# Probability times v in native fp32 for all 32 attention items, native scores for 4 items instead of 8

## The chip, the cores and the metric

The kernel runs on one core of one Trainium2 chip. The metric is device time in microseconds (us) from launch to end, as the median of several executions. A core has a matrix engine (TensorE, called PE in the rows; its weight loads are PEld), a vector engine (VectorE, DVE), a scalar engine (ScalarE, ACT), a third elementwise engine (GpSimd, POOL) and a sync engine (SyncE, SP), which here issues the transfers. Each engine runs its own list of instructions strictly in the order in which the program gives them and waits on semaphores for the others.

## The reference

Three stages follow each other: block-causal attention over 4 batches with 8 heads, 576 positions and a head width of 64, then two feed-forward layers on the 2304 tokens.

```python
scores = scale * np.matmul(q, k.transpose(0, 1, 3, 2))
mask = block_i >= block_j            # blocks of 64 positions
scores = np.where(mask, scores, -1000000000.0)
scores = scores - np.max(scores, axis=-1, keepdims=True)
attn = np.exp(scores)
attn = attn / (np.sum(attn, axis=-1, keepdims=True) + 1e-09)
x = np.matmul(attn, v)               # back to (2304, 512)
h = np.maximum(np.maximum(x @ w1, x @ w2), x @ w3)      # 512 -> 768
x = h @ w_out                                           # 768 -> 512
h = x @ w_in                                            # 512 -> 2048
out = (h * np.cos(h)) @ w_out2                          # 2048 -> 512
```

## The kernel before, in words

**Two ways to multiply.** A product of fp32 numbers is either made natively (both operands fp32; one matmul in the program is two passes in the trace) or from three products of fp32r parts: each operand is split into a high part (a cast to fp32r) and a low part (the rest), and high times high, low times high and high times low are added up in PSUM. The split costs a cast and a subtraction on ACT or DVE for each operand.

**Items.** Attention is cut into 32 items: batch, half, pair of heads. The low half of a batch has the query positions 0 to 319 (5 blocks of 64, keys in 3 tiles of 128), the high half the positions 320 to 575 (4 blocks, keys in 5 tiles). Items 0 to 3 are the low half of batch 0 (one for each pair), items 4 to 7 its high half, items 8 to 11 the low half of batch 1, and so on. The two heads of a pair stand side by side: rows 0 to 63 and 64 to 127.

**An item's steps.** `prep` splits q and k (tiles `qbd`, `kh`, `kl`) and v (`vs`) into parts. `scores` multiplies (PSUM tile `S`, one buffer), takes the row maximum (DVE, `stat`), the exponential (ACT, `prob`, one buffer for all items), the reciprocal of the row sums (DVE) and scales `prob`. `transposes` turns `prob` on PE (`tb`) and copies it to `pt`, as high and low part. `pv` multiplies v by `pt` into `X` and writes the result as high and low part (`xhi`, `xlo`), from which the first feed-forward layer reads.

**Native items.** The first 8 items (`NATIVE = 8`) do without any split: q is put by a transfer into a block-diagonal tile `qnat` (pool `cv_start`), scores are native, `pt` is one fp32 tile, and `pv` makes 64-column native matmuls, head 0 into rows 0 to 63 of `X`, head 1 into rows 64 to 127. For the other 24 items `pv` loads 128 columns of v parts, works on one head after the other, and adds the partial sums up in a tile `x32` (rows with `x<-X`).

**Weights.** `convert` takes a weight tile from its 64-bit words to high and low parts: about four DVE instructions of 128x512 (rows with `t`, then `wlo` or `vlo`) and one to three on either engine. 24 of them (`w1`, `w2`, `w3`, `wout`) are needed by the first layer.

**The first layer** (`moe1_units`) is a queue of units for each half of a batch: 18 groups of 12 matmuls (`psm<-xhi,whi` and the like, 4 units each) and 4 groups of 18. A group fills one of two PSUM banks (`ps_m`), which is emptied to a tile `hm` of the pool `wk`. The pool `wk` is opened in the place of `cv_start` (`R.close(cv_start)`, `wk = R.open(cv_start, ...)`): it comes into being when the last instruction that touches a tile of `cv_start`, `qnat` among them, is through.

**The order** of each engine's instructions is the work of a planner (class `Plan`): it records all instructions, prices them (`price`, `spent`), schedules the list forwards and backwards several times and emits the best order. `with R.unit()` makes several matmuls one piece that is not torn apart. The prices set only the order.

Of the kernel before, what the change touches and what calls it, by code (L numbers as in the profile page):

```python
# [8 lines left out]
F32 = mybir.dt.float32  # L9
F32R = mybir.dt.float32r  # L10
# [4 lines left out]
ALU = mybir.AluOpType  # L15
# [4 lines left out]
P = 128  # L20
NLOW, NHIGH = 320, 256
# [4 lines left out]
def f32(ap):  # L26
    return ap.bitcast(F32)
# [101 lines left out]

class Plan:  # L130
    CROSS = 150.0
    COLD = 30000.0
    EARLY = 130000.0
    WEIGHT = {"DVE": 2.5, "ACT": 1.0, "POOL": 100.0}

    def __init__(self, tc):
# [106 lines left out]
    def price(self, engine, method, outs, ins, kw):  # L243


        if engine == "SP":
            tiles = outs + ins
            return 600.0, 2000.0 + sum(v.n * v.rows * 4 for v in tiles[:1]) / 240.0, False
        n = outs[0].n
        if engine == "PE":  # L250
            late = 190.0
            if method == "transpose":
                return 109.0, late, False
            dt = ins[0].buf.dt
            if dt == F32:
                return 4 * n / 2.4 + 13, late, False
            load = ins[0].n / 1.2
            return (max(n / 2.4 + 3, 65.0) if dt == BF16 else max(n / 2.4 + 13.5, load)), late, False
        psum = any(v.buf.psum for v in outs + ins)
        if method == "tensor_reduce":  # L260
            n = ins[0].n
        spread = 120.0 * (outs[0].hi - outs[0].lo + 1 > n)
        if engine == "ACT":
            scaled = isinstance(kw.get("scale"), View)
            return (n * 0.833 + spread + (55 if psum else 100) + 95 * ("bias" in kw) + 95 * scaled
                    + 93 * ("accum_out" in kw)), 112.0, False
        if engine == "DVE":
            sb = [v for v in ins if not v.buf.psum]
            fast = method in ("tensor_copy", "tensor_scalar", "memset") and not psum
            two = method in ("tensor_tensor", "scalar_tensor_tensor") and len(sb) > 1  # L270
            if method == "reciprocal":
                return 70.0 + 5 * n, 100.0, False
            return n * (0.52 if fast else 1.04) + 68 + spread, 88.0, fast or two
        return (n * 3.3 + 75 if method == "tensor_tensor" else max(400.0, n * 1.04 + 195)), 45.0, method != "memset"
# [5 lines left out]
    def after(self, d, o, stop):  # L280
        if d.engine == "PE" and o.engine == "PE":
            return -d.late
        if d.engine == "CTL" or o.engine == "CTL":
            return 0.0
        return self.CROSS if stop > self.EARLY else 35.0

    def spent(self, o, start):
        return o.cost * (2 if o.engine == "PE" and start < self.COLD else 1)

    def forward(self, rank):  # L290

# [14 lines left out]
        def release(o):  # L306
# [5 lines left out]
            if o.ways:  # L312
                def done(way):
                    e, (cost, late, shared), _ = way
                    start = max(free[e] + load[e], at)
                    if shared:
                        start = max(start, port)
                    return start + cost * self.WEIGHT[e] + late
                chosen[o] = min(o.ways, key=done)
# [121 lines left out]
def fused_kernel(tc, qk, v2, w1, w2, w3, wout, w_in2, w_out2, out):  # L441
# [11 lines left out]
    R = Plan(tc)  # L453
# [7 lines left out]
    at = R.open(name="at", bufs=1, side="right")  # L461
    ps_x = R.open(name="ps_x", bufs=1, space=PSUM, side="right")
# [49 lines left out]
    for u in range(2):  # L512
        f = Half()
# [9 lines left out]
            ((4, 0, 0, 320, 1), (2, 0, 320, 192, 1), (3, 1, 0, 256, 1), (1, 1, 256, 128, 1), (0, 1, 384, 64, 1)),)  # L523
        HALF.append(f)
    POFF = {6: 0, 8: 4, 5: 9, 7: 12, 2: 2, 4: 6, 0: 16, 1: 0, 3: 4}
    NATIVE = 8

    items = []
    for b in range(B):
        for half in range(2):  # L530
            for pair in range(HP):
                it = Item()
                it.b, it.half, it.pair, it.n, it.f = b, half, pair, len(items), HALF[half]
                it.native = it.n < NATIVE
                items.append(it)
# [32 lines left out]
    def prep(it):  # L568
        f = it.f
        if it.native:  # L570
            return
        nb, nk = len(f.blocks), f.nk
        kh = it.kh = at.tile([P, S], F32R, "kh", tag="kh")[:, :nk]
        kl = it.kl = at.tile([P, S], F32R, "kl", tag="kl")[:, :nk]
        R.copy(kh, it.k)
        R.sub(kl, it.k, f32(kh))
        for a in (0, 64):
            q = it.q[a:a + 64].rearrange("p (b n) -> p b n", n=64)
            hi, lo = (t[a:a + 64, 0:nb, a:a + 64] for t in qbd)
            R.scale(hi, q, scale)  # L580
            R.vector.scalar_tensor_tensor(lo, q, scale, f32(hi), ALU.mult, ALU.subtract)
        vs = it.vs = at.tile([P, 5, 4, 64], F32R, "vs", tag="vs")
        js = slice(0, f.nj)
        R.copy(vs[:, js, 0:4:3], it.vr[:, js])
        R.sub(vs[:, js, 1:3], it.vr[:, js], f32(vs[:, js, 0:4:3]))

    def scores(it):

# [3 lines left out]
        for tile_ in f.tiles:  # L592
# [15 lines left out]
            for b, b0, c0, n, c in tile_:  # L608
                i = b - f.first
                part = s[:, :, c0:c0 + n] if c == 2 else s[:, b0, c0:c0 + n]  # L610
                R.vector.tensor_reduce(st[:, i:i + 1], part, axis=AX.XY if c == 2 else AX.X, op=ALU.max, negate=True)
                bias = st[:, i:i + 1]
# [15 lines left out]

    def transposes(it):
        order = it.f.order  # L630
        it.pt = at.tile([P, 2, 16, P], F32 if it.native else F32R, "pt", tag="pt")
        for c in range(0, len(order), 4):
            part = order[c:c + 4]
            n = P * len(part)
            t = ps_x.tile([P, 512], F32, "tb", tag="T", bufs=2)
            with R.unit():
                for x, (j, b) in enumerate(part):
                    o = (POFF[b] + j) * P
                    R.tensor.transpose(t[:, x * P:x * P + P], prob[:, o:o + P], ident)
            hi, lo = (it.pt[:, i, c:c + len(part)].rearrange("p b n -> p (b n)") for i in range(2))  # L640
            R.copy(hi, t[:, :n])
            if not it.native:
                R.vector.tensor_tensor(lo, t[:, :n], f32(hi), ALU.subtract)

    def pv(it):
        f = it.f
        n = f.n
        h, l = xhi[it.half][:, it.pair], xlo[it.half][:, it.pair]
        where = {}
        for c, (j, b) in enumerate(f.order):  # L650
            where.setdefault(j, []).append((c, b))
        if it.native:
            X = ps_x.tile([P, 512], F32, "X", tag="X", bufs=2)
        else:
            x32 = at.tile([P, NLOW], F32, "x32", tag="x32")
        for e in range(2):
            a, o = 64 * e, 64 - 64 * e
            if not it.native:
                X = ps_x.tile([P, 512], F32, "X", tag="X", bufs=2)
            for j in range(f.nj):  # L660
                c0, b0 = where[j][0]
                nb = len(where[j])
                q0 = 64 * (b0 - f.first)
                if not it.native and q0 >= f.both:

                    v = it.vs[:, j, 2 * e:2 * e + 2].rearrange("p a d -> p (a d)")
                    dst = X[:, f.both:2 * n - f.both].then(
                        lambda ap, q=q0 - f.both: ap.rearrange("p (c q) -> p c q", c=2)[:, :, q:])
                    dst.n = 2 * (n - q0)
                    R.tensor.matmul(dst, v, it.pt[:, :, c0:c0 + nb, a:a + 64], start=j == 0, stop=j == f.nj - 1,  # L670
                                    skip_group_check=True)
                    continue
                with R.unit():
                    for i in range(1 if it.native else 2):
                        p = it.pt[:, i, c0:c0 + nb, a:a + 64]
                        if it.native:
                            R.tensor.matmul(X[a:a + 64, q0:n], it.vr[:, j, e], p, start=j == 0,
                                            stop=j == f.nj - 1, skip_group_check=True)
                        else:
                            v = it.vs[:, j, 2 * e:2 * e + 2].rearrange("p a d -> p (a d)")  # L680
                            R.tensor.matmul(X[:, q0:n], v, p, start=j == 0 and i == 0, stop=j == f.nj - 1 and i == 1,
                                            skip_group_check=True)
            if not it.native:
                R.scalar.copy(x32[a:a + 64, :n], X[o:o + 64, :n])
                R.vector.tensor_tensor(x32[a:a + 64, :n], X[a:a + 64, :n], x32[a:a + 64, :n], ALU.add).cost += 118.0
                R.vector.tensor_tensor(x32[a:a + 64, f.both:n], X[a:a + 64, n:2 * n - f.both], x32[a:a + 64, f.both:n],
                                       ALU.add).cost += 118.0
        if it.native:
            R.copy(h, X[:, :n])
            R.vector.tensor_tensor(l, X[:, :n], f32(h), ALU.subtract)  # L690
        else:
            R.copy(h, x32[:, :n])
            R.sub(l, x32[:, :n], f32(h))


    bank_pools = [(ps_m, 2)]
# [106 lines left out]
    for n in range(NI + 1):  # L803
# [3 lines left out]
        for step in range(3):  # L807
# [4 lines left out]
            if step == 2 and n:  # L812
                it = items[n - 1]
# [122 lines left out]
    for n in range(len(seq) + LAG):  # L936
        if n < len(seq):
            c, fc = seq[n]
# [62 lines left out]
```

## Time and profile before

| | |
|---|---|
| median of 3 runs | 929.67 us (929.02 to 930.89) |
| the profiled execution | 929.6 us, its span from first to last instruction 927.5 us |
| PE busy | 899.2 us of the span (97%) |
| DVE, ACT busy | 662.7 us (71%), 478.7 us (52%) |
| mean granted clock | 0.994 |

The span is 2.1 us shorter than the execution's own time. The table's busy times include the latency of each instruction, so an engine that looks nearly full can still have room.

### The profile page before, as it was taken

How to read it: one execution, taken by the hardware profiler on the slowest of the kernel's cores; microseconds unless marked ns; L12 is line 12 of the kernel's file. 1: busy time of each engine (PE TensorE's matmuls, PEld its weight loads, DVE VectorE, ACT ScalarE, POOL GpSimd, SP SyncE). 2: the span in 40 equal slices, each digit the busy share in tenths (PEclk: the TensorE clock that was granted, in tenths of full speed). 3: DMA queues.
4: the chain of work that ended last, by engine and by line, in shares of the span. 5: the costliest groups of instructions: out<-in, count | busy, mean ns of one | idle time of the engine just before them, and what ended most of it. 6: DMA issues, size and time to landing. Idle time of an engine off the chain costs nothing.

```text
span 927.5 us, 14314 instructions
## 1 busy us (share of the span) xinstructions
PE 899.2 (97%) x5388; PEld 801.7 (86%) x5388; DVE 662.7 (71%) x1402; ACT 478.7 (52%) x1080; POOL 0.7 (0%) x7
## 2 busy tenths in 40 slices
PE   6888999999999999999999999999999999999998
PEld 5656989999999999999999988888888888888897
DVE  6979868999889887677776899855555555455554
ACT  5867457776767765766664553442224223322233
POOL 0000000000000000000000000000000000000000
PEclk9899999999999999999999999999999999999999
DMA  7455332442443421212003592220001000100010
GB/s 218 151 156 170 116 136 92 149 160 95 135 138 113 144 66 39 64 34 89 15 1 123 179 370 96 58 78 14 1 1 69 0 1 1 46 1 0 1 46 23
DMA packets 39492, 78.51 MB, mean 85 GB/s; under 512 B 9728, under 2 KB 20992, under 8 KB 39424
## 3 DMA queue, kind: packets, MB, share of 16 engines
q1 hardware_dynamic: 39424, 77.61, 25.3%
q8 instruction: 42, 0.69, 0.3%
q14 instruction: 26, 0.21, 0.1%
HBM read 61.34 MB, written 16.25 MB: 84 GB/s over the span
## 4 chain that ended last, share of the span: by engine, by line
PE 84%; DVE 9%; ACT 4%; issue 1%; DMA 1%; ACTq 0%; DVEq 0%; SPq 0%
PE psm L208 48%; PE po L208 21%; PE S L208 8%; ACT prob L208 4%; PE tb L208 3%; DVE stat L208 3%; PE X L208 3%; DVE t L208 2%; DVE x L208 1%; DVE pt L208 1%; DVE qbd L208 0%; DVE hm L208 0%; DMA qk<-qk 0%; DVE vs L208 0%; DVE wlo L208 0%
## 5 line engine op out<-in xcount | busy, mean ns | idle before, releaser
L208 PE MATMUL psm<-yh,w_in 128*128 128x512 f32 (+1 forms) x640 | 193.3, 368 | 0.0
L208 PE MATMUL psm<-xhi,whi 128*128 128x320 f32 (+1 forms) x576 | 177.3, 308 | 3.1 <-DVE hm L208 2.3
L208 PE MATMUL po<-w_out,gh 128*128 128x512 f32 x576 | 177.7, 390 | 0.0
L208 PE MATMUL psm<-xhi,wlo 128*128 128x320 f32 (+1 forms) x576 | 170.4, 296 | 0.0
L208 PE MATMUL psm<-xlo,whi 128*128 128x320 f32 (+1 forms) x576 | 170.2, 296 | 0.0
L208 ACT ACTIVATE th<-th,halfpi 128x512 f32<-128x512 f32 (+1 forms) x80 | 54.4, 682 | 187.9 <-DVE th L208 187.8
L208 PEld LDWEIGHTS psm<-yh,w_in 128*128 128x128 f32 x640 | 117.1, 188 | 20.5
L208 PEld LDWEIGHTS po<-w_out,gh 128*128 128x128 f32 x576 | 107.1, 188 | 21.4
L208 PE MATMUL psm<-yl,w_in 128*128 128x512 f32 (+1 forms) x320 | 117.7, 368 | 0.0
L208 PEld LDWEIGHTS psm<-xhi,whi 128*128 128x128 f32 x576 | 109.3, 190 | 6.2 <-DVE hm L208 4.5
L208 PE MATMUL po<-w_out,gl 128*128 128x512 f32 x288 | 112.0, 389 | 0.0
L208 PEld LDWEIGHTS psm<-xlo,whi 128*128 128x128 f32 x576 | 109.3, 190 | 0.1
L208 PEld LDWEIGHTS psm<-xhi,wlo 128*128 128x128 f32 x576 | 109.0, 189 | 0.0
L208 ACT ACTIVATE prob<-S,stat 128x128 f32<-128x128 f32 (+8 forms) x144 | 74.8, 526 | 55.2 <-DVE stat L208 50.7
L208 DVE TENSOR_SCALAR th<-psm 128x512 int32<-128x512 f32 (+1 forms) x80 | 50.8, 637 | 69.0 <-PE psm L208 69.0
L208 DVE TENSOR_REDUCE stat<-S 128x1 f32<-128x320 f32 (+8 forms) x144 | 64.8, 484 | 48.4 <-PE S L208 34.8
L208 DVE TENSOR_TENSOR th<-psm,th 128x512 f32<-128x512 f32 (+1 forms) x80 | 50.9, 637 | 51.6 <-ACT th L208 51.5
L208 DVE TENSOR_TENSOR gl<-th,gh 128x512 fp32r<-128x512 f32 (+1 forms) x80 | 50.8, 636 | 35.0 <-ACT gh L208 34.7
L208 PEld LDWEIGHTS psm<-yl,w_in 128*128 128x128 f32 x320 | 60.3, 188 | 10.7
L208 ACT CAST gh<-th 128x512 fp32r<-128x512 f32 (+1 forms) x76 | 43.7, 575 | 49.9 <-DVE th L208 49.4
L208 PEld LDWEIGHTS po<-w_out,gl 128*128 128x128 f32 x288 | 54.0, 188 | 11.3
L208 PE MATMUL tb<-ident,prob 128*128 128x128 f32 x400 | 60.2, 277 | 2.0 <-ACT pt L208 0.8
(87 smaller groups left out, 1520.8 us busy)
## 6 DMA issues: line engine op xcount, KB each, us to landing
raw<-w SPq DMA_DIRECT2D x18, 512.0 KB, 3.9
raw<-w_in SPq DMA_DIRECT2D x16, 512.0 KB, 3.6
raw<-w_out SPq DMA_DIRECT2D x16, 512.0 KB, 3.6
vr<-v SPq DMA_DIRECT2D x16, 320.0 KB, 3.3
qk<-qk SPq DMA_DIRECT2D x12, 416.0 KB, 3.3
kept_in<-both SPq DMA_DIRECT2D x9, 512.0 KB, 2.6
w_in<-kept_in SPq DMA_DIRECT2D x9, 512.0 KB, 9.6
out<-osb SPq DMA_DIRECT2D x18, 256.0 KB, 2.0
```

The costliest lines, as they stand in the source:

```text
L208: return lambda: getattr(real, method)(*[value(a) for a in args], **{k: value(a) for k, a in kw.items()})
```

## The change

`NATIVE` goes from 8 to 4: scores of items 4 to 7 are now made from fp32r parts, so that their q and k are split on ACT and DVE. The probability product is native for all items: `vs`, the low part of `pt` and `x32` are gone, and `xhi` and `xlo` are made from `X` directly. The two heads' matmuls of an item form one unit and take turns (head 0 and head 1 of one key tile, then of the next). The planner's prices change too: no doubled PE price in the first 30 us, half the price for native matmuls onto 64 rows and 295 ns for each such unit, and a higher rate for transfers.

```diff
 class Plan:
-    COLD = 30000.0
+    SWITCH = 295.0
...
-            return 600.0, 2000.0 + sum(v.n * v.rows * 4 for v in tiles[:1]) / 240.0, False
+            return 600.0, 2000.0 + sum(v.n * v.rows * 4 for v in tiles[:1]) / 330.0, False
...
-                return 4 * n / 2.4 + 13, late, False
+                return (4 * n / 2.4 + 13) / (2 if outs[0].rows == 64 else 1), late, False
...
     def spent(self, o, start):
-        return o.cost * (2 if o.engine == "PE" and start < self.COLD else 1)
+        return o.cost
...
-    NATIVE = 8
+    NATIVE = 4
...
-        vs = it.vs = at.tile([P, 5, 4, 64], F32R, "vs", tag="vs")
-        js = slice(0, f.nj)
-        R.copy(vs[:, js, 0:4:3], it.vr[:, js])
-        R.sub(vs[:, js, 1:3], it.vr[:, js], f32(vs[:, js, 0:4:3]))
...
-            hi, lo = (it.pt[:, i, c:c + len(part)].rearrange("p b n -> p (b n)") for i in range(2))
-            R.copy(hi, t[:, :n])
-            if not it.native:
-                R.vector.tensor_tensor(lo, t[:, :n], f32(hi), ALU.subtract)
+            R.copy(it.pt[:, c:c + len(part)].rearrange("p b n -> p (b n)"), t[:, :n])
...
+        X = ps_x.tile([P, 512], F32, "X", tag="X", bufs=2)
+        with R.unit():
             for j in range(f.nj):
                 c0, b0 = where[j][0]
                 q0 = 64 * (b0 - f.first)
+                for e in range(2):
+                    a = 64 * e
+                    p = it.pt[:, c0:c0 + len(where[j]), a:a + 64]
+                    R.tensor.matmul(X[a:a + 64, q0:n], it.vr[:, j, e], p, start=j == 0, stop=j == f.nj - 1,
                                     skip_group_check=True)
+            R.unit_op.cost += R.SWITCH
+        R.copy(h, X[:, :n])
+        R.vector.tensor_tensor(l, X[:, :n], f32(h), ALU.subtract)
```

Three places show how the lists move. The first is ACT's list around the first emptying of a first-layer bank (`hm<-psm`). Before, it stands among the exponentials of item 7 (`stat_186`), after both of that item's first reductions:

```order
L208 ACTIVATE prob,stat_186<-S,stat_186 128x576
L208 ACTIVATE prob,stat_186<-S,stat_186 128x448
L208 ACTIVATE raw<-raw 128x512
L208 COPY pt<-tb 128x512
L208 CAST whi_676<-t 128x512
L208 COPY hm<-psm 128x320
```

After the change it stands with item 4 (`stat_199`):

```order
L208 ACTIVATE prob,stat_199<-S,stat_199 128x512
L208 CAST xhi_299<-X 128x320
L208 ACTIVATE prob,stat_199<-S,stat_199 128x384
L208 ACTIVATE qbd_104<-qk 64x4x64
L208 CAST whi_490<-t 128x512
L208 ACTIVATE raw<-raw 128x512
L208 COPY hm<-psm 128x320
```

It moved forward by three items. The second place is PE's list in the high half of batch 0. Before, one item (5) runs from one score tile to the next with no first-layer matmul in between:

```order
L208 MATMUL tb<-ident,prob 128x128 x12
L208 MATMUL X<-pt,vr 64x256
L208 MATMUL tb<-ident,prob 128x128 x4
L208 MATMUL X<-pt,vr 64x256 x4
L208 MATMUL S<-qk,qnat_83 128x512
L208 MATMUL S<-qk,qnat_83 128x384
L208 MATMUL X<-pt,vr 64x256
L208 MATMUL X<-pt,vr 64x192
L208 MATMUL X<-pt,vr 64x64
```

After, the second score tile of item 6 stands in pieces between first-layer matmuls, of which the first three of twelve are shown:

```order
L208 MATMUL S<-kh,qbd_104 128x384
L208 MATMUL S<-kl,qbd_104 128x384
L208 MATMUL S<-kh,qbd_111 128x384
L208 MATMUL psm<-xhi_299,whi_657 128x320
L208 MATMUL psm<-xlo_303,whi_657 128x320
L208 MATMUL psm<-xhi_299,wlo_754 128x320
```

They are closed by item 5's probability product as one unit, with equal matmuls of the two heads side by side:

```order
L208 MATMUL psm<-xhi_299,whi_657 128x320
L208 MATMUL psm<-xlo_303,whi_657 128x320
L208 MATMUL psm<-xhi_299,wlo_754 128x320
L208 MATMUL X<-pt,vr 64x256 x6
L208 MATMUL X<-pt,vr 64x192 x2
L208 MATMUL X<-pt,vr 64x64 x2
```

Ahead of the last matmul of item 7's product the list before has 246 first-layer matmuls, and 24 of these stand ahead of item 7's second score tile. The list after has 201 ahead of item 7's product and 252 ahead of item 10's. The third place is PE's list at the product of item 8. Before:

```order
L208 MATMUL X<-pt,vs 128x320 x2
L208 MATMUL X<-pt,vs 128x384
L208 MATMUL X<-pt,vs 128x2x64
L208 MATMUL X<-pt,vs 128x320 x2
L208 MATMUL X<-pt,vs 128x384
L208 MATMUL X<-pt,vs 128x2x64
```

After (the scores ahead of it are item 9's):

```order
L208 MATMUL S<-kl,qbd_104 128x64
L208 MATMUL S<-kh,qbd_111 128x64
L208 MATMUL X<-pt,vr 64x320 x2
L208 MATMUL X<-pt,vr 64x192 x2
L208 MATMUL X<-pt,vr 64x64 x2
L208 MATMUL psm<-hh,vhi 128x320
```

Eight matmuls on 128 columns of v parts became six native ones on 64 columns.

## Rows read from the trace of the kernel before

**Rows 1.** The page: busy time of the engines

```profile
PE 899.2 (97%) x5388; PEld 801.7 (86%) x5388; DVE 662.7 (71%) x1402; ACT 478.7 (52%) x1080; POOL 0.7 (0%) x7
```

**Rows 2.** Busy time by stretch: us, PE, PEld, DVE, ACT, POOL, clock, DMA

```profile
0.00:25.00 25.00, 15.86 (x77) 12.78 (x77) 17.73 (x55) 14.48 (x38) 0.73 (x7) 1.00 0.69 202
25.00:84.40 59.40, 49.41 (x255) 32.62 (x255) 51.22 (x138) 44.55 (x111) 0.00 (x0) 0.91 0.51 161
0.00:91.70 91.70, 72.40 (x378) 52.21 (x379) 76.25 (x208) 63.98 (x159) 0.73 (x7) 0.94 0.55 173
84.40:128.30 43.90, 42.74 (x288) 39.77 (x285) 37.55 (x86) 24.70 (x57) 0.00 (x0) 1.00 0.36 118
```

**Rows 3.** The same columns, instructions on the banks psm alone

```profile
0.00:84.40 84.40, 11.26 (x56) 9.73 (x56) 0.00 (x0) 0.43 (x1) 0.94 0.56 174
84.40:128.30 43.90, 36.46 (x228) 33.48 (x228) 6.32 (x13) 1.88 (x5) 1.00 0.36 118
```

**Rows 4.** Timeline, PE and ACT: start, us, instruction, count [idle before]

```profile
82.16 1.77 PE L208 MATMUL S<-qk,qnat 128*128 128x512 f32 x4 [0.57 <-ACT prob L208]
...
83.97 0.43 ACT L208 COPY hm<-psm 128x320 f32<-128x320 f32 x1 [0.31 <-PE S L208]
...
84.45 0.41 PE L208 MATMUL psm<-xhi,whi 128*128 128x320 f32 x1
```

**Rows 5.** Timeline of DVE: the reciprocals of a low item and of item 7

```profile
33.71 0.18 DVE L208 RECIPROCAL stat<-stat 128x5 f32<-128x5 f32 x1
...
91.72 0.17 DVE L208 RECIPROCAL stat<-stat 128x4 f32<-128x4 f32 x1
```

**Rows 6.** Timeline of PE: native products (121.42 whole, then single passes), first-layer neighbours

```profile
37.52 1.21 PE L208 MATMUL X<-pt,vr 128*64 128x320 f32 x12
...
80.50 1.09 PE L208 MATMUL X<-pt,vr 128*64 128x256 f32 x8
...
121.19 0.30 PE L208 MATMUL psm<-hh,vlo 128*128 128x320 f32 x1
121.42 1.08 PE L208 MATMUL X<-pt,vr 128*64 128x256 f32 x4
...
121.91 0.38 PE L208 MATMUL X<-pt,vr 128*64 128x256 f32 x1
...
122.12 0.38 PE L208 MATMUL X<-pt,vr 128*64 128x256 f32 x1
...
122.43 0.41 PE L208 MATMUL psm<-hh,vhi 128*128 128x320 f32 x1
122.68 0.31 PE L208 MATMUL psm<-hl,vhi 128*128 128x320 f32 x1
122.83 0.31 PE L208 MATMUL psm<-hh,vlo 128*128 128x320 f32 x1
...
123.50 2.44 PE L208 MATMUL X<-pt,vr 128*64 128x256 f32 x16
```

**Rows 7.** Timeline of PE, products and scores from parts, and four transposes

```profile
113.82 0.60 PE L208 MATMUL tb<-ident,prob 128*128 128x128 f32 x4
...
144.85 1.27 PE L208 MATMUL X<-pt,vs 128*128 128x320 f32 x8
145.97 0.33 PE L208 MATMUL psm<-xhi,whi 128*128 128x256 f32 x1
...
151.21 0.31 PE L208 MATMUL S<-kh,qbd 128*128 128x320 f32 x1
...
152.92 0.28 PE L208 MATMUL S<-kh,qbd 128*128 128x64 f32 x1
...
493.56 2.07 PE L208 MATMUL X<-pt,vs 128*128 128x512 f32 x10
495.47 0.36 PE L208 MATMUL psm<-hh,vhi 128*128 128x320 f32 x1
```

**Rows 8.** Longest wait of PE from 128.3 to 500: us, times, longest

```profile
PE psm L208 <- DVE hm L208: 2.1, 3, 1.3
```

More of the change, by code (lines that the diff above doesn't have):

```diff
@@ L630, in transposes @@
         order = it.f.order
-        it.pt = at.tile([P, 2, 16, P], F32 if it.native else F32R, "pt", tag="pt")
+        it.pt = at.tile([P, 16, P], F32, "pt", tag="pt")
         for c in range(0, len(order), 4):
@@ L651, in pv @@
             where.setdefault(j, []).append((c, b))
[L652 to L659, printed above, removed]
+        X = ps_x.tile([P, 512], F32, "X", tag="X", bufs=2)
+        with R.unit():
             for j in range(f.nj):
@@ L661, in pv @@
                 c0, b0 = where[j][0]
-                nb = len(where[j])
                 q0 = 64 * (b0 - f.first)
[L664 to L670, printed above, removed]
-                                    skip_group_check=True)
-                    continue
@@ L673, in pv @@
[L673 to L693, printed above, removed]
+                for e in range(2):
+                    a = 64 * e
+                    p = it.pt[:, c0:c0 + len(where[j]), a:a + 64]
+                    R.tensor.matmul(X[a:a + 64, q0:n], it.vr[:, j, e], p, start=j == 0, stop=j == f.nj - 1,
+                                    skip_group_check=True)
```

## Prediction

> **What bounds the kernel now.** I start with the page's busy times: PE is busy for 899 of 927.5 us [rows 1], so PE is the bound, yet a busy time includes each instruction's latency and does not say where PE runs at its pace. The table by stretch does, read by counts. From 25 to 84.4 us PE gets 255 matmul records into 59.4 us, 4.3 per us, at a mean granted clock of 0.91 (full clock is 2.4 GHz; part of the stretch ran at 1.2). From 84.4 to 128.3 it gets 288 into 43.9 us, 6.6 per us, at full clock [rows 2]. The reader should see that the first 84 us are thin, and the filtered table says what is missing there: 56 records on the banks `psm`, of which 32 are the 16 warm-up matmuls (two passes each), so 24 first-layer matmuls; afterwards 228 in half the time [rows 3].
>
> What keeps the first layer out is in the timeline. Two banks are full, and the first `hm` copy that would empty one starts at 83.97, when the second score tile of item 7, the last to read `qnat`, is through; 0.5 us later the first layer flows [rows 4]. That is the pool rule of the code: `hm` lives in `wk`, `wk` takes the place of `cv_start`, and `qnat` lives in `cv_start`. DVE is the next engine behind PE there: busy for 76.25 of the first 91.7 us, of which it lacks 7.3 in the first 25 us and 8.2 after [rows 2]. After 128.3 us PE is fed: its longest wait in sum, for DVE's `hm`, is 2.1 us up to 500 us [rows 8].
>
> **Part 1: native scores for 4 items.** `qnat` is free after item 3. In the list after, the first `hm` copy stands with item 4, and 201 instead of 24 first-layer matmuls stand ahead of item 7's product or second tile. At 0.15 us each (122.68 to 122.83 [rows 6]) the 177 are 27 us of PE work that moves into the thin stretch. It is not all gained: the weights must be converted for it, and DVE gets the splits of items 4 to 7 as well.
>
> So the place to time is item 10's product, behind which the list after has 252 more matmuls of the first layer in a row, with little else: from there PE is fed. What it waits for is the eleventh reciprocal on DVE. I counted DVE's list, with 0.60 us for a whole 128x512 instruction and the others scaled by size (an estimate, put right by the next figures). Up to the eighth reciprocal the list before has 73.8 us: 88 conversion instructions 43.4, 36 row maxima 16.2, the rest 14.2. By the trace that is at 91.72 [rows 5], with DVE busy for 76.25 [rows 2], so my prices are 3% low. The list after has 77.3 us up to its eighth, and 106.5 up to its eleventh: 110 conversion instructions 55.1 (22 weights), 51 row maxima 22.9, q and k splits 10.6, `hm`, `hl`, `hh` 6.9, the rest 10.9. Times 1.033 that is 110.0 us busy. In the first 25 us DVE does 17.7 [rows 2]; 92.3 remain. Without any idle time the eleventh reciprocal comes at 117.3. With the idle share of before (8.2 of 66.7 us after the first 25, 12%) it comes at 130. I take 122.5, an idle share of 5%, since each high item now brings more DVE work (13 us instead of about 9 by my counts) and DVE's gaps were those of the chain of one item. From a low item's reciprocal to its product 3.8 us pass (33.71 [rows 5] to 37.52 [rows 6]); I say 4. Item 10's product starts at 126.5, between 121 and 134.
>
> **Part 2: the native product.** Heads in turn run side by side. A single head's four passes of 256 columns take 1.08 us at 121.42, with the last one's latency. Eight passes of both heads, at 80.50, take 1.09: twice the work in the same time. A low item's twelve passes take 1.21 us at 37.52 [rows 6]. One head's passes of 256 columns start 0.21 apart (121.91 and 122.12 [rows 6]), 0.83 us per 1000 columns; a low item's 2x576 columns per head are 0.96 us and a high item's 2x1024 are 1.71.
>
> Entering and leaving costs extra: from 121.19 to 122.68 are 1.49 us; taking off two first-layer matmuls of 0.15 and four passes of 0.21 leaves 0.35 [rows 6]. So a low item takes 1.31 and a high one 2.06, against 1.12 (144.85 to 145.97) and 1.91 (493.56 to 495.47) from parts [rows 7]. The product alone is slower on PE, by 0.19 and 0.15, 4 us over 24 items.
>
> The Trainium skill, page "TensorEngine Tiling", section "Key Properties", says that a change of tiling mode drains the engine while a change of tile does not, and that tiles run independently. By that rule each unit pays two drains and none between the heads, and the sum is the same 4 us; the page has no price for a drain, and the 0.35 us above is this trace's. Were a change of tile a drain too, the sum would be that of the last rival below.
>
> **Part 3: the relief of DVE and ACT.** The low parts of `pt`, `vs` and the sums in `x32` go. They lie beside PE work today, so their price is what PE waits for: 2.1 us for `hm` after 128.3 [rows 8]. I take all of it, with 0 as the other bound (a copy can come late for another reason); 1 more for the waits just ahead of 128.3, where 1.2 of 43.9 us are not busy [rows 2].
>
> **The sum.** Before, item 7's product ends at 125.9 (123.50 plus 2.44 [rows 6]); 801.6 us of the span follow. After, what follows the start of item 10's product has, by the lists: 6 first-layer matmuls less (-0.9), 27 transposes less (0.60 for four with latency, so 0.11 to 0.15 each [rows 7]: -3), the scores of three low items less (151.21 to 152.92, 1.7 each [rows 7]: -5.1), two products less but 22 dearer ones (10 x 1.31 + 12 x 2.06 = 37.8 against 12 x 1.12 + 12 x 1.91 = 36.4: +1.4), and 3 us of waits less: 791 us. The span is 126.5 + 791 = 917.5. The profiled execution took 929.6, 2.1 above its span and at the median of the runs (929.67), so I add 2.1: 919.6. One thing pulls below that: PE at half clock for some of the thin stretch (mean 0.91 [rows 2]), which first-layer work between the items should keep at 2.4 GHz. 9% of the level's range of a half is 18% of 59.4 us, 10.7 us at half clock with up to 5 us lost; some of that is on an item's chain, and I take 1.5. That gives **918**. Bounds: 121 + 791 + 2.1 - 5 = 909 and 134 + 794 (no wait goes) + 2.1 = 930.
>
> **Rivals.** *More gain:* DVE is kept full, ACT takes more of the copies, the clock stays up, and the first 25 us lose 3 us less: 909 less 3, 906. For it: ACT has room (64 of 91.7 us [rows 2]). Against: one buffer each of `S` and `prob` leaves gaps whatever DVE has to do. *The start does not get shorter:* each item is still a chain through PE, DVE and ACT, and PE's list now has first-layer matmuls between the links, each behind a wait on a weight; an idle share of 14% on DVE puts the product at 136 and the time at 929 or 930, no change. For it: DVE's idle share was as large after 84.4, with PE full (6.3 of 43.9 [rows 2]). *The heads do not overlap* (slower): if the hardware runs them one behind the other, as the single-head passes at 121.42 do, a low item costs 0.96 and a high one 1.71 more, 30 us over the 22 items after that place (10 and 12), and the time is 948. It decides once more than 0.4 of the overlap is lost (12 of 30 us). Against: both overlapped stretches [rows 6]. *A drain at each change of head* (slower): 5 or 9 changes more per item at up to 0.35, over the 22 items after that place (10 low, 12 high), are 55 us: 973; the eight passes at 80.50 speak against it.
>
> **Chances.** Forecast, 910 to 927: 0.70. More gain: 0.14. No shorter start, 927 to 935: 0.11 (a third each faster, same, slower by 0.2%, which is about what a measurement here can tell from no change: 1.9 us). No overlap 0.03, drains 0.02. Faster 0.88, same 0.04, slower 0.08. The range runs from 906 to 930, which holds the forecast and about half of each of the next two.
>
> **What would show it.** In the profile after: the first `hm` copy near 45 to 55 us instead of 83.97; well over 150 first-layer matmuls by 90 us; the eleventh reciprocal at 117 to 130 and item 10's product right after; pairs of `X` passes a few ns apart, a low item in about 1.3 us and a high one in about 2.05 from neighbour to neighbour; 0 to 2 us of waits for `hm` later on; the last 400 us as before. The prediction is wrong if the start is bound by the items' chain rather than DVE's work, in either direction, or if the 0.35 us at each unit is larger among other neighbours.

## The result and the profile after

The changed kernel takes 919.47 us (median of 4 runs, 918.92 to 922.57), the kernel before 930.10 in the same session. The ratio is 0.9893, 95% interval [0.9868, 0.9918]: 10.6 us faster. The prediction said 918, between 906 and 930. The profiled execution took 919.06 us, with a span of 917.3.

The page's busy times of the kernel after answer to [rows 1]:

```profile
PE 892.8 (97%) x5580; PEld 794.9 (87%) x5580; DVE 557.0 (61%) x1167; ACT 464.5 (51%) x1047; POOL 0.7 (0%) x7
```

DVE lost 106 us of work, ACT 14, PE 6. DVE's 106 us are no measure of the gain: the time fell by a tenth of it. By stretch, with the columns of [rows 2] (us, PE, PEld, DVE, ACT, POOL, clock, DMA):

```profile
0.00:25.00 25.00, 17.35 (x75) 15.27 (x77) 16.28 (x48) 17.01 (x45) 0.74 (x7) 0.86 0.66 195
25.00:84.40 59.40, 53.38 (x373) 46.20 (x370) 53.52 (x133) 50.84 (x123) 0.00 (x0) 0.97 0.49 158
84.40:128.30 43.90, 39.17 (x286) 34.32 (x285) 41.18 (x102) 41.54 (x110) 0.00 (x0) 0.96 0.47 152
```

and the instructions on the banks `psm` alone, as in [rows 3]:

```profile
0.00:84.40 84.40, 33.85 (x176) 29.39 (x176) 3.35 (x7) 1.66 (x4) 0.94 0.54 169
84.40:128.30 43.90, 17.80 (x105) 15.32 (x104) 2.43 (x5) 0.88 (x2) 0.96 0.47 152
```

Read by counts, the stretch from 25 to 84.4 holds 373 matmul records instead of 255, and 144 first-layer matmuls (176 less the 32 warm-up passes) run before 84.4 us instead of 24. The stretch behind it is no longer all first layer: 105 records on `psm` instead of 228, since items 6 to 9 now stand among them. The reader should also see the ACT column: 41.54 of 43.9 us, where it was 24.70. In that stretch DVE and ACT are now both nearly full (41.18 and 41.54), and PE is busy for less of it than before (39.17 us, it was 42.74).

The single instructions, ACT's first `hm` copy, then DVE's reciprocals of item 7 and item 10 (the eighth and the eleventh):

```profile
47.73 0.40 ACT L208 COPY hm<-psm 128x320 f32<-128x320 f32 x1
```

```profile
94.85 0.16 DVE L208 RECIPROCAL stat<-stat 128x4 f32<-128x4 f32 x1
...
124.57 0.18 DVE L208 RECIPROCAL stat<-stat 128x5 f32<-128x5 f32 x1
```

and PE's timeline: start, us, instruction, count, [idle before <- what ended it]. 114.79, 121.46 and 129.18 are the products of items 8, 9 and 10; 174.93 and 206.56 are a low and a high item's product in the fed part:

```profile
112.13 0.41 PE L208 MATMUL S<-kh,qbd 128*128 128x320 f32 x1 [2.37 <-ACT prob L208]
112.38 0.31 PE L208 MATMUL S<-kl,qbd 128*128 128x320 f32 x1
112.53 0.40 PE L208 MATMUL S<-kh,qbd 128*128 128x320 f32 x2
...
113.13 0.40 PE L208 MATMUL S<-kl,qbd 128*128 128x256 f32 x1
113.32 0.52 PE L208 MATMUL S<-kh,qbd 128*128 128x256 f32 x2
...
114.79 2.05 PE L208 MATMUL X<-pt,vr 128*64 128x320 f32 x12
...
121.46 1.20 PE L208 MATMUL X<-pt,vr 128*64 128x320 f32 x12
124.14 0.41 PE L208 MATMUL S<-kh,qbd 128*128 128x320 f32 x1 [1.48 <-ACT prob L208]
...
129.18 1.20 PE L208 MATMUL X<-pt,vr 128*64 128x320 f32 x12
...
174.72 0.28 PE L208 MATMUL psm<-hh,vlo 128*128 128x256 f32 x1
174.93 1.20 PE L208 MATMUL X<-pt,vr 128*64 128x320 f32 x12
176.06 0.41 PE L208 MATMUL psm<-xhi,whi 128*128 128x320 f32 x1
176.31 0.31 PE L208 MATMUL psm<-xlo,whi 128*128 128x320 f32 x1
...
206.29 0.34 PE L208 MATMUL S<-kh,qbd 128*128 128x384 f32 x1
206.56 1.96 PE L208 MATMUL X<-pt,vr 128*64 128x256 f32 x20
208.44 0.42 PE L208 MATMUL psm<-xhi,whi 128*128 128x320 f32 x1
208.70 0.31 PE L208 MATMUL psm<-xlo,whi 128*128 128x320 f32 x1
```

The waits of PE over the whole span (us, times, longest), the largest row, in the kernel before and in the kernel after:

```profile
PE S L208 <- ACT prob L208: 9.9, 9, 2.0
```

```profile
PE S L208 <- ACT prob L208: 12.5, 7, 3.7
```

and from 128.3 to 500 us, against [rows 8]:

```profile
PE psm L208 <- DVE hm L208: 1.2, 3, 0.8
```

where the kernel before has this second row:

```profile
PE psm L208 <- ACT hm L208: 1.2, 2, 0.7
```

PE's longest waits are those of a score tile for ACT, before and after, and nearly all in the start: `S` has one buffer, and the next item's scores wait until the exponential has read it. After 128.3 us the wait for DVE's `hm` fell from 2.1 to 1.2, and the 1.2 for ACT's `hm` went.

### The profile page after: what moved, and what is told of

Its sections match the earlier page's. It is cut to its first block, busy times and chain, and to the rows that moved or that the text cites. A ratio compares the mean times of both kernels' runs of the same rounds, so it can differ in the third digit from the quotient of the medians.

```text
span 917.3 us, 14412 instructions
## 1 busy us (share of the span) xinstructions
PE 892.8 (97%) x5580; PEld 794.9 (87%) x5580; DVE 557.0 (61%) x1167; ACT 464.5 (51%) x1047; POOL 0.7 (0%) x7
## 4 chain that ended last, share of the span: by engine, by line
PE 87%; ACT 6%; DVE 4%; issue 1%; DMA 1%; ACTq 0%; POOLq 0%; POOL 0%; DVEq 0%
PE psm L208 51%; PE po L208 21%; PE S L208 8%; PE tb L208 4%; ACT prob L208 4%; PE X L208 4%; DVE stat L208 2%; DVE t L208 1%; DMA raw<-w_out 1%; ACT raw L208 0%; ACT qbd L208 0%; ACT pt L208 0%; ACT t L208 0%; DVE hm L208 0%; DVE kl L208 0%
## 5 line engine op out<-in xcount | busy, mean ns | idle before, releaser
L208 ACT ACTIVATE prob<-S,stat 128x128 f32<-128x128 f32 (+8 forms) x144 | 74.9, 527 | 56.6 <-DVE stat L208 50.3
L208 PE MATMUL S<-kh,qbd 128*128 128x288 f32 (+8 forms) x312 | 73.3, 306 | 7.5 <-ACT prob L208 5.9
L208 DVE TENSOR_TENSOR hm<-psm,hm 128x320 f32<-128x320 f32 (+1 forms) x96 | 43.5, 453 | 58.1 <-PE psm L208 44.1
```

Source lines behind the costliest of these rows:

```text
L208: return lambda: getattr(real, method)(*[value(a) for a in args], **{k: value(a) for k, a in kw.items()})
```

## The experiments

Twelve kernels; the kernel before took 929.5 to 930.5 us beside them. "Item 10" is the start of its product on PE, "reciprocal" the eleventh on DVE, both in us. "DVE" is the work on it up to that reciprocal (the first 25 us and the rest added) and its idle share after the first 25 us, both from tables by stretch.

| kernel | us | ratio [95%] | first `hm` | reciprocal | item 10 | DVE, idle |
|---|---|---|---|---|---|---|
| after | 919.47 | 0.9893 [0.9868, 0.9918] | 47.7 | 124.6 | 129.2 | 107.3, 9% |
| 8 native items | 932.93 | 1.0040 [1.0026, 1.0053] | 88.0 | | | |
| 8 native items, `qnat` moved | 918.00 | 0.9877 [0.9860, 0.9895] | 44.6 | 120.0 | 126.0 | 103.1, 12% |
| before, 4 native items | 940.58 | 1.0120 [1.0105, 1.0134] | 51.1 | 150.9 | | 133.8, 9% |
| the same, new prices | 944.43 | 1.0157 [1.0143, 1.0171] | 49.7 | 154.7 | | 133.1, 10% |
| before, new prices | 927.28 | 0.9974 [0.9963, 0.9985] | 87.2 | | | |
| after, more DVE work | 938.74 | 1.0084 [1.0067, 1.0102] | 54.8 | 131.4 | 142.4 | 110.2, 12% |
| after, less DVE and ACT work | 910.64 | 0.9794 [0.9781, 0.9807] | 43.4 | | | |
| after, heads apart | 945.11 | 1.0170 [1.0155, 1.0185] | 49.6 | 132.2 | 136.8 | |
| after, old prices | 938.13 | 1.0090 [1.0077, 1.0103] | 56.0 | 137.7 | | 116.3, 13% |
| after, product priced as before | 929.59 | 1.0001 [0.9992, 1.0010] | 50.3 | 129.5 | | 111.4, 10% |
| after, first 30 us priced as before | 922.31 | 0.9919 [0.9905, 0.9932] | 48.8 | 130.0 | | |
| 12 native items, `qnat` moved | 914.17 | 0.9822 [0.9804, 0.9841] | 48.1 | 119.4 | 125.1 | 100.6, 10% |

The theory is the prediction's: `wk` opens early because `qnat` is done early, and then the DVE work of the first items sets the start. Where the list puts item 10 or its reciprocal in another place among first-layer work, the field is empty.

### Native items and the pool of `qnat`

The first kernel is the changed one with 8 native items; the second also moves `qnat` out of the pool whose closing holds `wk` up.

```diff
-    NATIVE = 4
+    NATIVE = 8
```

> The changed kernel with native scores for 8 items again, all else as changed. Theory 1 (the gain comes from opening the tiles of the first layer at item 3 instead of item 7): the first hm copy goes back to about 80 us, under 40 first-layer matmuls stand ahead of item 7's product, and the time is 930 us (926 to 934), the gain is gone; 4 us of dearer products and some 3 us of waits saved cancel. Theory 2 (the gain comes from the relief of DVE and ACT by the native product): 919 to 923 us.

```diff
-    qnat = [cv_start.tile([P, 5, P], F32, f"qnat{i}") for i in range(2)]
+    qnat = [at.tile([P, 5, P], F32, f"qnat{i}") for i in range(2)]
...
-    NATIVE = 4
+    NATIVE = 8
```

> The changed kernel with native scores for 8 items, but with qnat in the pool of the attention tiles, so that the first layer's tiles don't wait for it. Theory 1: the gain stays without the cut to 4 items, 918 us (914 to 922), first hm copy near 48 us; DVE saves 6 us of splits for items 4 to 7, PE pays 3 us more for native scores. Rival (native scores of items 4 to 7 were the cost, by PE time or by their chain): 926 to 931 us.

With 8 native items in the old pool, the time is 932.93: the native product and its lighter DVE list bring nothing by themselves. ACT's timeline shows the same late copy as [rows 4]; its wait ends with item 7's scores:

```profile
88.01 0.42 ACT L208 COPY hm<-psm 128x320 f32<-128x320 f32 x1 [2.48 <-PE S L208]
```

Only 24 first-layer matmuls stand ahead of that. With `qnat` in another pool, the copy comes 3.2 us earlier than in the changed kernel and the eleventh reciprocal 4.6. From this kernel's ACT and DVE timelines:

```profile
44.56 0.43 ACT L208 COPY hm<-psm 128x320 f32<-128x320 f32 x1 [0.85 <-PE psm L208]
```

```profile
120.02 0.18 DVE L208 RECIPROCAL stat<-stat 128x5 f32<-128x5 f32 x1
```

Both came out as the theory said. The same 8 native items give 932.93 and 918.00, by the pool alone. So `NATIVE = 4` works through the time at which `wk` opens, and not through how the scores of items 4 to 7 are made. What the move of `qnat` alone would do to the kernel before, with its products from parts, was not run.

### The changed item count without the native product

First with the prices of before, then with the new ones (`SWITCH` has no unit to stand on there). Both leave `pv`, `vs` and the low part of `pt` as before.

```diff
-    NATIVE = 8
+    NATIVE = 4
```

> The kernel before with native scores for 4 items, products from parts for items 4 to 31 and the old prices. The early opening comes, but DVE gets the splits and the low parts of items 4 to 7 on top (about 5 us a high item, 4 a low one, some 30 us up to item 10). Theory 1 with a start bound by DVE's work: the gain is mostly eaten, 928 us (924 to 935). Rival (the early opening alone makes the gain, DVE has room for it): 916 to 920 us.

> Native scores for 4 items and the planner's new prices, but the products of items 4 to 31 from parts as before (the changed kernel without its first half). With the old prices this took 940.6 us. Theory 1 (the native product is needed because DVE has no room in the start): 932 us (927 to 938), later than with 8 native items. Rival (the 940.6 was the old prices alone): 917 to 922 us.

Both were slower than expected, 940.58 and 944.43. The early opening takes place (51.1 and 49.7 us), and yet the eleventh reciprocal is at 150.9 and 154.7. Their rows by stretch, 84.4 to 128.3 us, first the one with the old prices, then the new:

```profile
84.40:128.30 43.90, 30.56 (x165) 26.21 (x164) 40.49 (x87) 35.99 (x81) 0.00 (x0) 0.82 0.37 117
```

```profile
84.40:128.30 43.90, 34.55 (x189) 31.07 (x189) 40.55 (x86) 36.53 (x82) 0.00 (x0) 0.85 0.42 132
```

DVE is as full as in the changed kernel (40.5 of 43.9), PE gets 165 and 189 records instead of 286, at clocks of 0.82 and 0.85. The reason is in DVE's list: up to the eleventh reciprocal it holds 22 low parts of `pt`, 20 sums into `x32`, and `vs`, which the changed kernel has not. That is 26 us more work on DVE (133 against 107), and the reciprocal is 26 and 30 us later. The second of the two also rules out the old prices as the cause of the first's loss.

### DVE's load in the first layer's conversions

More: two shifts by 0 bits of 128x512 words per conversion of the 24 first-layer weight tiles. Less: the low words of these 24 tiles are left out, which takes one addition from DVE and one scaling from ACT (or DVE) out of each; the weights of that kernel lack their low words.

```diff
-    def convert(src, hi, lo, pool, bufs):
+    def convert(src, hi, lo, pool, bufs, extra=False):
...
+        if extra:
+            for _ in range(2):
+                R.vector.tensor_scalar(i32(t), i32(t), 0, None, ALU.logical_shift_left)
...
```

> The changed kernel with two more DVE instructions of 128x512 (a shift by nothing) in each of the 24 weight conversions of the first layer, 0.66 us each conversion, known to the planner. Theory (DVE's work sets the place of item 10's product): 14.5 us more work ahead of the eleventh reciprocal, which comes at 135 to 139 us instead of 124.6, and the time is 930 us (926 to 934). Rival (the chain of each item sets it, DVE has room): 920 to 923 us.

```diff
-        R.scale(low, low.bitcast(U32), 2.0 ** -29)
+        if not less:
+            R.scale(low, low.bitcast(U32), 2.0 ** -29)
...
-        R.vector.tensor_tensor(i32(t), i32(t), low, ALU.add).cost += 275.0
+        if not less:
+            R.vector.tensor_tensor(i32(t), i32(t), low, ALU.add).cost += 275.0
...
```

> The changed kernel without the low words of the 24 first weight tiles: each conversion leaves out one DVE addition (0.6 us) and one ACT scaling (0.57 us), so the weights are rounded a little differently. Theory (the work of DVE and ACT sets the start): 13 us less on each engine up to item 10, and the time is 910 us (905 to 914). Rival (the chain of each item and the planner's order set it, so that the longer time of the kernel with more DVE work was the order's doing): 916 to 921 us.

More work: 938.74 (six runs from 934.70 to 939.48), where 930 was expected; the direction held and the loss was nearly twice as large. A shift takes 0.42 us in this trace. Up to the eleventh reciprocal DVE's work is only 2.9 us more, since the list put 20 conversions there instead of 23 and the others behind it; the rest of the loss lies in the idle share (12% instead of 9%) and behind item 10. The rows by stretch show where:

```profile
100.00:125.00 25.00, 19.81 (x122) 17.65 (x121) 20.02 (x53) 18.20 (x51) 0.00 (x0) 0.80 0.43 130
125.00:150.00 25.00, 19.23 (x102) 16.48 (x101) 20.58 (x52) 19.62 (x55) 0.00 (x0) 0.73 0.46 140
```

PE is at 0.80 and 0.73 of its clock there, and in the second stretch only 102 records run. Less work: 910.64 against an expected 910, with PE fed from 84.4 on:

```profile
84.40:128.30 43.90, 42.39 (x332) 39.78 (x332) 33.82 (x83) 31.23 (x79) 0.00 (x0) 1.00 0.45 148
```

So less elementwise work in the start shortens the time by what the count of work said. Its list is another one, though: item 10's product stands behind 492 first-layer matmuls there, at 149.0 us, and no longer marks where PE becomes fed. The other direction is weaker evidence. The loss of 19.3 us does not follow from 2.9 us more work ahead of the reciprocal: item 10's product has 225 first-layer matmuls ahead of it instead of 252, and item 11's follows at 151.1 with 240 ahead, where the changed kernel has 576 ahead of it. The planner's order moved with the work, and these runs do not separate the two. The second kernel takes work from ACT as well as DVE; which of the two counts more was not separated either.

### The heads, one after the other

```diff
-            for j in range(f.nj):
-                c0, b0 = where[j][0]
-                q0 = 64 * (b0 - f.first)
-                for e in range(2):
-                    a = 64 * e
+            for e in range(2):
+                a = 64 * e
+                for j in range(f.nj):
+                    c0, b0 = where[j][0]
+                    q0 = 64 * (b0 - f.first)
```

> The changed kernel with the same units, prices and order of units, but in each probability product first all matmuls of head 0, then all of head 1. Theory (taking turns is what lets the heads overlap): in the kernel before a high item's product in this order took about 1.3 us more than the two heads side by side would, a low one 0 to 0.5 more, so 16 high items make 21 and 16 low ones 0 to 8 us: 942 us (932 to 950). Rival (the engine overlaps the heads in either order, as the low items' 1.21 us at 37.52 before suggests): 919 to 923 us.

945.11 against 942 expected. The same matmuls in another order within each unit cost 25.6 us. The product of a high item that starts at 199.65 in this kernel, PE on tile `X` alone in three equal stretches (a pass that lies across a border counts in both):

```profile
199.65:200.73 1.08, 1.08 (x5) 1.00 0.76 190
200.73:201.81 1.08, 1.08 (x10) 1.00 0.69 281
201.81:202.89 1.08, 1.08 (x8) 1.00 0.11 42
```

The changed kernel's item that starts at 206.56, first of two stretches:

```profile
206.56:207.64 1.08, 1.08 (x10) 0.77 (x12) 0.00 (x0) 0.00 (x0) 1.00 0.02 8
```

With the heads in turn ten passes fall into the first 1.08 us; apart, five. Overlap comes only in the middle, where the end of head 0 and the start of head 1 stand near each other in the list. The neighbours of a low and of a high item's product in the kernel with the heads apart:

```profile
182.53 0.28 PE L208 MATMUL psm<-hh,vlo 128*128 128x256 f32 x1
...
184.71 0.31 PE L208 MATMUL psm<-xlo,whi 128*128 128x320 f32 x1
...
199.38 0.34 PE L208 MATMUL S<-kh,qbd 128*128 128x384 f32 x1
...
203.13 0.32 PE L208 MATMUL psm<-xlo,whi 128*128 128x320 f32 x1
```

By the method below a high item costs 3.43 us instead of 2.09, a low one 1.91 instead of 1.32; for 16 of each that is 31 us. The sum is above the 25.6 measured. Item 10's product comes 7.6 us later (136.8), close to the 8.9 that the ten products ahead of it add; behind its start the span is 17.9 us longer, where the 22 products make 22.0. What takes up the other 4 us is not shown. The Trainium skill, page "TensorEngine Tiling (Array Packing)", section "Key Properties", says that different tiles can execute in parallel. The rows agree with it and add a condition: here they did so only when the list set their matmuls side by side.

### The planner's prices

All four prices put back to those of before, then two of them alone:

```diff
-    SWITCH = 295.0
+    SWITCH = 0.0
+    COLD = 30000.0
...
-                return (4 * n / 2.4 + 13) / (2 if outs[0].rows == 64 else 1), late, False
+                return 4 * n / 2.4 + 13, late, False
...
-        return o.cost
+        return o.cost * (2 if o.engine == "PE" and start < self.COLD else 1)
...
-            return 600.0, 2000.0 + sum(v.n * v.rows * 4 for v in tiles[:1]) / 330.0, False
+            return 600.0, 2000.0 + sum(v.n * v.rows * 4 for v in tiles[:1]) / 240.0, False
```

> The changed kernel with the planner's old prices (PE doubled in the first 30 us, 240 for transfers, no halving for 64 rows, no price for the switch). Theory 1: the prices matter little, 920 us (917 to 924). Rival (the better order is a fruit of the prices): 925 to 930 us.

The product's price alone (the first two pairs of lines):

> The changed kernel with the native product priced as before (no halving for 64 rows, nothing for the switch), all other prices new. The kernel with all old prices took 938 us. Theory (a product priced about twice too dear makes the planner put transposes and scores too early behind it, all through the attention): 932 us (928 to 938). Rival (the doubled PE price of the first 30 us, or the rate of transfers, made the 938): 919 to 923 us.

The doubled PE price in the first 30 us alone (the third pair):

> The changed kernel with only the doubled PE price of the first 30 us put back. Between the changed kernel (919.5) and all old prices (938.1) the price of the product made 10 us. Theory: the doubled price makes most of the other 8.5, in the first 100 us, 925 us (922 to 930). Rival (transfer rate, or the prices act only together): 918 to 921 us.

And the new prices on the kernel before:

> The kernel before with the planner's new prices (no doubled PE price, 330 for transfers, half the price for native matmuls onto 64 rows), native scores for 8 items and products from parts as before. Theory 1 (the opening of the first layer's tiles is the gain): the first hm copy stays near 80 us and the time is 927 us (923 to 931). Rival (the prices are the gain): 917 to 921 us.

Here the theory fell: I had thought the prices worth next to nothing, and the changed kernel with the old ones takes 938.13, slower than before the change. The work is the same; 18.7 us lie in its order and in which of DVE and ACT takes a copy. Of these the product's price accounts for 10.1 and the first 30 us for 2.8; the other 5.7 belong to the transfer rate, which was not tried alone, or to prices acting together. The 2.8 were expected to be most of what the product's price leaves over, and they are hardly clear of noise: the intervals of the two ratios overlap. On the kernel before, the new prices are worth 2.4 us by the ratio (0.26%), and the first `hm` copy stays late there (87.2), as expected.

With the product priced too high, other instructions stand where their inputs are not there yet. In the kernel with the old product price, PE's waits from 128.3 to 500 us:

```profile
PE tb L208 <- ACT prob L208: 3.0, 10, 0.7
PE psm L208 <- ACT hm L208: 2.9, 2, 1.7
```

The transposes wait ten times for the scaled `prob`, in the changed kernel once (0.2 us). All waits of PE in that stretch are 7.4 us instead of 2.3, half of the 10.1; where the other half lies stays open. With all old prices it is 13 times and 3.7 us, and the clock from 25 to 50 us is 0.69:

```profile
25.00:50.00 25.00, 18.05 (x98) 13.85 (x98) 20.24 (x63) 18.59 (x51) 0.00 (x0) 0.69 0.47 153
```

### A faster version

The runs suggest moving `qnat` and, since native scores spare DVE the splits, making more items native:

```diff
-    qnat = [cv_start.tile([P, 5, P], F32, f"qnat{i}") for i in range(2)]
+    qnat = [at.tile([P, 5, P], F32, f"qnat{i}") for i in range(2)]
...
-    NATIVE = 4
+    NATIVE = 12
```

> The changed kernel with native scores for 12 items instead of 4, their native q and k held in a pool of their own, so that the weight pool opens as early as in the changed kernel (as in the run with 8 native items that took 918.0). Theory (VectorE and ScalarE work of the first 130 us sets the start, TensorE's own work the rest): the splits of q and k of items 4 to 11 fall away, so the eleventh reciprocal comes before the 120.0 us of that run, at 113 to 118; TensorE's pay for it is some tenths of a us for each item. Time 916 (913 to 919). Rival (TensorE already sets the end of the start when 8 items are native, and more native scores only lengthen its work, at the lower clock that the start has): 919 to 923, with the eleventh reciprocal no earlier than 120.

914.17 us, ratio 0.9822 [0.9804, 0.9841], 5 us below the changed kernel, the fastest here but for the one that leaves work out. The time is as expected and the way to it only in part. The reciprocal is not at 113 to 118:

```profile
119.41 0.18 DVE L208 RECIPROCAL stat<-stat 128x5 f32<-128x5 f32 x1
```

It is 0.6 us earlier than with 8 native items, which is nearly what the rival said, though DVE has 2.5 us less to do. Item 10's product is 0.9 earlier; the rest of the 3.3 us between the two spans comes after it. From 128.3 to 500 us PE waits for `hm` 0.4 us in this trace, against 1.6 with 8 native items. What of that is the number of native items and what another order, stays open.

## Why the prediction was right

**Early opening of `wk`: right.** First `hm` copy predicted at 45 to 55, measured 47.7; 156 first-layer matmuls stand ahead of the product that starts at 87.2, for "well over 150 by 90 us". The two kernels with 8 native items show that it is the pool: with `wk` open early, how the scores of items 4 to 7 are made moves the time by no more than the intervals can tell (918.00 and 919.47).

**The DVE count: right, with errors that cancel.** Predicted was the eleventh reciprocal at 122.5 from 110.0 us of work, 17.7 of it in the first 25 us, and 5% idle after that. Measured: 124.57 from 107.3 us (16.28 and 90.99), 9% idle. The work was 2.7 us less than counted, the first 25 us did 1.4 less of it, and the idle share cost 3.4 us more. Item 10's product started at 129.2 instead of 126.5, inside the 121 to 134 given. The idle share is what I had chosen, not derived, and it was the weakest term: over the eight kernels of the table it is 9 to 13%, close to the 12% of [rows 2] for the kernel before, which I had discounted. The reason given was more DVE work per item, which should have filled the gaps that the chain of one item had left. Those gaps did shrink, but others came. DVE's largest waits, before from 25 us to the eighth reciprocal, after from 25 us to the eleventh:

```profile
DVE stat L208 <- PE S L208: 6.2, 7, 1.6
```

```profile
DVE stat L208 <- ACT prob L208: 3.0, 5, 1.4
DVE t L208 <- ACT t L208: 1.9, 4, 1.1
```

Before, DVE waited for PE's scores (after: 1.8 us); now it waits above all for ACT, which has filled up too (41.54 of 43.9 us). The prediction did not look at ACT except as room for copies. That ACT's load is the cause of these waits is argued from its busy time; no run changed ACT alone.

**The price of the native product: right.** Predicted 1.31 us for a low item and 2.06 for a high one. Measured, from the neighbours: 174.72 to 176.31 less 0.12 and 0.15 for the neighbours themselves is 1.32; 206.29 to 208.70 less 0.17 and 0.15 is 2.09. The prediction's 1.12 and 1.91 for the parts [rows 7] leave out what entering and leaving costs there. The neighbours of the same two products in the kernel before:

```profile
144.73 0.28 PE L208 MATMUL psm<-xhi,wlo 128*128 128x256 f32 x1
...
146.14 0.29 PE L208 MATMUL psm<-xlo,whi 128*128 128x256 f32 x1
...
493.42 0.31 PE L208 MATMUL psm<-hh,vlo 128*128 128x320 f32 x1
...
495.67 0.31 PE L208 MATMUL psm<-hl,vhi 128*128 128x320 f32 x1
```

Measured in the same way they are 1.17 (1.41 less twice 0.12) and 1.95 (2.25 less twice 0.15), so the loss on PE is 0.15 us per item, somewhat less than the 0.19 and 0.15 of the prediction. The no-overlap rival was false for this order, and the kernel with the heads apart shows that it would have decided: there 1.34 of a high item's 1.71 and 0.59 of a low one's 0.96 are lost, and it takes 945.11.

**The relief of DVE: right in the total, under-stated in the text.** The step priced it at 3 us, by PE's waits behind the start. There it held: behind item 7's product before (125.9 us) PE waits 5.0 us in all, behind the start of item 10's product after 2.3, of which the waits for DVE's `hm` make 0.9 less and those for ACT's 1.2. Whether the relief or the new order of the list brought that, no run separates. The larger worth lies in the start: without the native product the same item count takes 944.43, so the native product is worth 25 us there, and the eleventh reciprocal comes 30 us later. The sum had this, since the DVE list that was counted no longer held those instructions, but a reader of the step would have thought `NATIVE = 4` useful by itself. It costs 17 us (927.28 to 944.43).

**The remainder: right.** Predicted 791 us of span behind the start of item 10's product, measured 917.3 - 129.2 = 788.1. With the 2.7 us lost ahead of it, the span comes to 0.2 under the 917.5 of the sum, before the 1.5 taken off for the clock. That closeness is luck: two errors of nearly 3 us cancel. The counts of matmuls in the sum are those of the trace, and the waits fell as the sum had it, so the 2.9 lie elsewhere; where, is not shown. The clock term did not come: the mean rose from 0.91 to 0.97 between 25 and 84.4, but fell to 0.86 in the first 25 us and 0.96 after 84.4, where [rows 2] have 1.00.

**What was missing: the prices.** They were told of as setting only the order, and got no term. They are worth 18.7 us to the changed kernel. The forecast did not suffer, because every number was read from the list that the new prices made; had I forecast from the diff alone, it would have. The worth of the pool (14.9 us), of the native product (25.0) and of the prices (18.7) do not add up to a gain of 10.6, because each is what is lost when that part alone is missing, and `NATIVE = 4` has a cost of its own.

## What to carry to other kernels

When a pool takes the place of another, find the last reader of the old one and what waits for the new: here moving the two `qnat` tiles was worth 15 us (932.93 to 918.00) in the kernel with native products; with products from parts it was not tried. When an engine sets the pace through a chain of items, count its work from the changed list, and bound its idle share by what other traces of the same stretch show: here 5% was chosen, 12% was that of the trace before, and 9% came. An order made from prices is part of a change: the same work at the old prices was slower than the kernel before.

## What the runs showed of the hardware

**Half clock after a wait, and not at once.** In the changed kernel PE idled for 2.37 us before 112.13, then ran at full pace (matmuls of 320 columns 0.15 apart at 112.38), and after that at half: the product at 114.79 takes 2.05 us, where one of the same size takes 1.20 at 121.46. The granted clock in a stretch that begins 1.2 us after that wait, and in one that begins as a later wait of 1.48 us ends (the stretch, its length, PE's busy time and records, the clock, then two numbers on transfers; a clock of 1.00 is 2.4 GHz):

```profile
113.30:116.50 3.20, 3.20 (x17) 0.50 0.51 164
124.10:128.30 4.20, 4.08 (x31) 1.00 0.23 67
```

For 3.2 us the granted clock is 0.50, the lower of the two levels, 1.2 GHz, while PE is busy throughout; that is worth about 1.6 us (an estimate: half of the 3.2). The wait of 1.48 us before 124.14 was followed by no such fall, and item 10's product took 1.20 us. The two cases differ in more than the length of the wait: ahead of the first lay another of 0.44 us with a single transpose between them. So a late item can cost more than its wait. That may be a part of why the kernels with a starved PE (clock 0.73 to 0.85 in the rows above) lost more than was expected of them; how large a part was not measured.

**Two heads' native passes side by side.** In the changed kernel's product at 206.56 the two heads' passes start 6 to 7 ns apart, and the pairs 0.22 us apart (256 columns). In the kernel with the heads apart one head's passes alone start 0.22 us apart, so a pair takes as long as a single pass.
